# Gated linear attention with a top-1 expert layer on one core: the floor of a decay total moved into its scan, and two small VectorE operations moved to GpSimd

## The chip, the core and the metric

One core of one Trainium2 chip runs the whole program: attention, routing and the expert layer. The metric is device time in microseconds (us) of one launch. Engines are named as in the profile: PE is TensorE, PEld its weight loads, DVE VectorE, ACT ScalarE, POOL GpSimd, SP SyncE, from which most DMAs are issued.

## The reference

```
q, k, v, alpha: (4, 8, 768, 48) float32        # alpha between 0.8 and 1.0
for t in range(768):
    state = alpha[:, :, t, :, None] * state + k[t] (outer) v[t]     # 48 x 48 per head
    y[:, :, t] = q[t] @ state
x = y rearranged to (3072 tokens, 384)
logits = x @ w_gate (384 x 8) + modality_bias[modality_id]
e = argmax(logits);  gate = softmax(logits)[e]
out = gate * (relu(x @ w1[e]) @ w2[e])         # w1: 384 x 1024, w2: 1024 x 384, 8 experts
```

## The kernel before

**Attention in chunks.** The 3072 tokens are 24 chunks of 128: chunk `i` is batch `i // 6`, place `i % 6` in its sequence. A chunk holds all eight heads, laid out as four pairs of 48 rows padded to 64. Instead of stepping through time, the kernel takes within a chunk the running product of alpha and its reverse, scales k and q by them, and does the rest with matmuls. Between chunks of one batch a state `S` (four pairs of 48 x 48) is handed on.

**One loop, software pipelined.** Loop step `s` works on several chunks at once: `decay(s)`, `scale_k(s-1)`, `scale_q(s-1)`, `keys(s-2)`, `scores(s-2)`, `combine(s-3)`, `outputs(s-4)`, `rows(s-4)`. In the order of one step:

- `decay` (L236 on) runs on DVE. A scan backwards along time (L240) writes `G`: each element is x times the element before it in the scan, plus `DR`. `DR` is 0 except for a 1 at each of the five segment borders, where x is 0, so that the product starts again from 1. The first column of each of the four segments is the decay of the state over the whole chunk, the total. L244 writes these four totals, not below 1e-30, to `amin[:, i]`; L245 takes their reciprocal into `d`; L246 is the forward scan `Fw`, started from it.
- `scale_k` (L262) and `scale_q` (L268) multiply transposed k and q, read from PSUM, by `G` and `Fw` on DVE.
- `scores` (L277) multiplies them on PE, ACT copies the result to `scT` (L281), and POOL zeroes the future half in place with two affine selects (L282).
- `combine`: if the chunk isn't the first of its batch, L304 writes `U` (tiles `UB0` and `UB1` in turn), the state `S` times the totals in `G`. Then PE runs three runs of matmuls into one PSUM tile `y`: L324 (`U` by q), L330 (new k by v, for the state), L334 (scores by v). L338 then makes the next state on DVE, `S = U + ` the new part. L340 is the same for the first chunk of a batch.
- `outputs` (L347, ACT) copies `y` to `yt`; `rows` (L357 on PE, L361 and L362 on ACT) turns it and writes it to DRAM; `logits_turned` (L369) and `logits` (L378, L380) make the expert logits for two chunks at a time.

**Routing** for groups of finished chunks (`GROUPS`) runs between them on DVE with small matmuls (L433 to L477). Two experts are fixed early, after 16 and 18 chunks (`route_early`, L539 to L578): DVE writes the expert's number to `meta` (L545), SP reads it and issues the 3 MB of that expert's weights (`w1r`, `w2r`), and POOL gathers 256 token rows (`xg`, L679) and their gates (`gg`, L684) by indirect DMAs. The gates of the first 18 chunks go to DRAM as `gd` (L674) before they are gathered.

**Expert layer.** From about 170 us on, 12 slots of 256 tokens run: weights are split on ACT and DVE (L897, L899) into a high and a low part, and three matmuls take the place of one (L925 to L927, L948 to L950). POOL scatters the results.

**What sets the order.** A scheduler that works from a timeline of its own places the instructions of DVE and POOL from the dependencies; PE's matmuls in the later loop steps are pinned to the order in which they are written. Each engine then takes its list strictly from the front: an instruction that waits holds back all that stand behind it on that engine. POOL's list holds the affine selects and the indirect DMAs.

`out_of_range` (L698) reads all of `amin` after the last `decay`, and a fallback runs if a total is under 1e-17.

Of the kernel before, what the change touches and what calls it, by code (L numbers as in the profile page):

```python
# [14 lines left out]
ALU = mybir.AluOpType  # L15
# [7 lines left out]
B, H, S, D = 4, 8, 768, 48  # L23
NC = S // P
NP = H // 2
SEG = P + 1
# [22 lines left out]
AFLOOR = 1.0e-30  # L49
# [5 lines left out]
def attention_moe(ctx: ExitStack, tc: tile.TileContext, q, k, v, alpha, mid, wg, mb, w1, w2, out):  # L55
    nc = tc.nc
    vec, act, pool, pe, sp = nc.vector, nc.scalar, nc.gpsimd, nc.tensor, nc.sync
# [63 lines left out]
    def pin(ins):  # L121

        if mark.get("pin"):
            tc.keep_in_program_order(ins)
        return ins
# [24 lines left out]


    DR = ac.tile([P, NP * SEG + 1], F32, name="DR")
    vec.memset(DR, 0.0)
    vec.memset(DR[:, SEG :: SEG], 1.0)
    X, DF, UB = [], [], []
    for i in range(2):
# [12 lines left out]
    amin = ac.tile([P, NU, NP], F32, name="amin")  # L169
# [66 lines left out]
    def decay(i):  # L236
        x, d = X[i % 2], DF[i % 2]
        Fw = sb.tile([P, NP * SEG], F32, name="Fw", bufs=3)
        G = sb.tile([P, NP * SEG + 1], F32, name="G", bufs=4)
        vec.tensor_tensor_scan(  # L240
            G[:, 1:][:, ::-1], x[:, 1:][:, ::-1], DR[:, 1:][:, ::-1], 0.0, op0=ALU.mult, op1=ALU.add
        )
        ac1 = amin[:, i]
        vec.tensor_scalar(ac1, G[:, 1::SEG], AFLOOR, None, op0=ALU.max)  # L244
        vec.reciprocal(d[:, 0::SEG], ac1)  # L245
        vec.tensor_tensor_scan(Fw, x[:, :-1], d, 0.0, op0=ALU.mult, op1=ALU.add)  # L246
        st[i, "G"], st[i, "F"] = G, Fw

# [47 lines left out]
    def combine(i):  # L296
        c = i % NC
        qh, vt, sc = st[i, "q"], VT[i % NV], st[i, "s"]
        U = UB[i % 2]
        halves = [slice(64 * g, 64 * g + 64) for g in range(2)]  # L300
        if c > 0:
            S0 = st[i, "S"]
            A = st[i, "G"][:, 1::SEG].unsqueeze(2).broadcast_to([P, NP, D])
            vec.tensor_tensor(U[:, :, :D], S0, A, op=ALU.mult)  # L304

        yk = ps.tile([P, 2, 512], F32, name="y")

        def y(r, j):
            return yk[r, j % 2, P * (j // 2) : P * (j // 2 + 1)]

        kv = yk[:, 1, 2 * P : 2 * P + NP * D].rearrange("p (j d) -> p j d", j=NP)
        fresh = {(o, g) for o in range(2) for g in range(2)}

        def first(o, g):
            new = (o, g) in fresh
            fresh.discard((o, g))
            return new

        if c > 0:
            for a in range(2):  # L320
                for o in range(2):
                    for g in range(2):
                        x, j = g ^ o, 2 * a + o
                        pin(pe.matmul(y(halves[x], j), U[halves[g], j], qh[halves[g], j], start=first(o, x), stop=False))  # L324
        if c < NC - 1:
            kn = st[i, "n"]
            for h in range(H):
                j = h // 2
                r = halves[h % 2]
                pin(pe.matmul(kv[r, j], kn[:, j, r], vt[:, h, :D], start=first(1, h % 2), stop=False))  # L330
        for j in range(NP):
            for x, r in enumerate(halves):
                g = x ^ j % 2
                pin(pe.matmul(y(r, j), vt[:, 2 * j + g], sc[g][:, j], start=first(j % 2, x), stop=(j > 1)))  # L334
        if c < NC - 1:
            S1 = sb.tile([P, NP, D], F32, name="S")
            if c > 0:
                vec.tensor_tensor(S1, U[:, :, :D], kv, op=ALU.add)  # L338
            else:
                vec.tensor_copy(S1, kv)  # L340
            st[i + 1, "S"] = S1
        st[i, "yp"] = yk
# [454 lines left out]
    for s in range(NU + 3):  # L797
# [16 lines left out]
        if s < NU:  # L814
            decay(s)
# [25 lines left out]
        if 0 <= s - 3 < NU:  # L841
            combine(s - 3)
# [242 lines left out]
```

## Time and profile before

| what | us |
|---|---|
| median of 3 runs | 410.47 |
| lowest and highest | 408.89, 410.51 |
| the profiled execution | 408.91 |
| its span, first to last instruction | 407.1 |
| attention with most of the routing | 0 to about 170 |
| expert layer | about 170 to 400 |

The profiled execution is one run: its time is 1.81 us more than its span, which is what lies around the first and last instruction. Line numbers are those of the kernel before. A row of the timeline reads: start in us from the span's start, duration in us, engine, line, operation, output and inputs, shape, count, and in brackets how long the engine was idle before it and what released it. A row of the groups gives total busy us and mean ns of one, and after the second bar the idle time before. A row of the stages gives a stretch, its length, each engine's busy time and count, then the granted TensorE clock, the DMA share and GB/s.

### The profile page before, as it was taken

To read this page: it belongs to the slowest core of one execution; us is meant where nothing else is said; L and a number is where in the kernel's file an instruction comes from. 1 tells how busy PE (TensorE), PEld (TensorE's weight loads), DVE (VectorE), ACT (ScalarE), POOL (GpSimd) and SP (SyncE) were. 2 spreads that over 40 slices of the span, in tenths; PEclk is the share of its full clock that TensorE was granted. 3 is DMA by queue.
4 is the path that set the end of the run, shared out by engine and by line. 5 is a ranking of instruction groups with operands and counts; after the bars stand their busy time and mean duration, and the time that the engine had idled before them with its cause. 6 is when DMAs were issued, how large, how long until landed. Compare 5 with 4: busy or idle time off the path is not lost. (4 is left out here: it accounts for less than half of the span.)

```text
span 407.1 us, 9558 instructions
## 1 busy us (share of the span) xinstructions
PE 378.2 (93%) x3659; PEld 347.7 (85%) x3659; DVE 278.2 (68%) x550; ACT 224.3 (55%) x425; POOL 137.3 (34%) x175
## 2 busy tenths in 40 slices
PE   3898999999999888899997999999999999999992
PEld 3777787788778666778997999999999999999992
DVE  6787889878979965587689566665656666554230
ACT  3467677567566435344586657475654656545230
POOL 9321321321222233402657515244351634232010
PEclk9999999999999989999998999999999999999998
DMA  6999988579675096505999786566867657420010
GB/s 129 209 202 214 201 184 192 127 165 199 138 160 117 26 360 210 204 22 163 385 370 331 252 283 202 198 220 203 268 197 264 210 195 238 148 106 35 6 42 10
DMA packets 132655, 75.12 MB, mean 185 GB/s; under 512 B 103777, under 2 KB 120222, under 8 KB 132600
## 3 DMA queue, kind: packets, MB, share of 16 engines
q1 hardware_dynamic: 128504, 64.57, 56.6%
q0 software_dynamic: 4096, 9.85, 7.0%
q8 instruction: 31, 0.51, 0.5%
q14 instruction: 24, 0.20, 0.1%
HBM read 64.95 MB, written 9.65 MB: 183 GB/s over the span
## 5 line engine op out<-in xcount | busy, mean ns | idle before, releaser
L925 PE MATMUL tr<-xH,w1H 128*128 128x256 f32 x264 | 74.7, 286 | 1.3 <-DVE hL L932 1.3
L926 PE MATMUL tr<-xL,w1H 128*128 128x256 f32 x264 | 75.1, 285 | 0.0
L927 PE MATMUL tr<-xH,w1L 128*128 128x256 f32 x264 | 74.9, 285 | 0.0
L282 POOL TENSOR_SCALAR_AFFINE_SELECT scT<-scT 128x512 f32<-128x512 f32 x48 | 35.2, 754 | 107.1 <-ACT scT L281 107.1
L948 PE MATMUL sc<-w2H,hH 128*128 128x384 f32 x192 | 65.4, 342 | 1.0 <-ACT hH L929 1.0
L949 PE MATMUL sc<-w2L,hH 128*128 128x384 f32 x192 | 64.6, 337 | 0.0
L899 DVE TENSOR_TENSOR w2L<-w2r,w2H 128x768 fp32r<-128x768 f32 x52 | 49.1, 956 | 21.9 <-ACT w2H L897 21.0
L950 PE MATMUL sc<-w2H,hL 128*128 128x384 f32 x192 | 63.6, 340 | 0.0
L866 POOL DMA_INDIRECT out_dram<-os,odx x24 | 27.6, 1148 | 89.2 <-ACT os L953 34.9
L899 DVE TENSOR_TENSOR w1L<-w1r,w1H 128x768 fp32r<-128x768 f32 x44 | 41.7, 956 | 21.3 <-ACT w1H L897 20.6
L897 ACT CAST w1H<-w1r 128x768 fp32r<-128x768 f32 x44 | 36.0, 834 | 29.8 <-PE tr L926 23.0
L925 PEld LDWEIGHTS tr<-xH,w1H 128*128 128x128 f32 x264 | 50.9, 194 | 1.6 <-issue 1.6
L926 PEld LDWEIGHTS tr<-xL,w1H 128*128 128x128 f32 x264 | 51.2, 194 | 0.0
L927 PEld LDWEIGHTS tr<-xH,w1L 128*128 128x128 f32 x264 | 51.1, 194 | 0.0
L679 POOL DMA_INDIRECT xg<-xd,idx x26 | 32.0, 1230 | 42.5 <-PE y L887 36.5
L897 ACT CAST w2H<-w2r 128x768 fp32r<-128x768 f32 x52 | 42.2, 834 | 7.0 <-PE sc L950 6.8
L932 DVE SCALAR_TENSOR_TENSOR hL<-tr,hH 128x512 fp32r<-128x512 f32 x46 | 31.5, 686 | 10.5 <-ACT hH L929 7.2
L948 PEld LDWEIGHTS sc<-w2H,hH 128*128 128x128 f32 x192 | 36.1, 188 | 2.4 <-ACT hH L929 1.2
L929 ACT ACTIVATE hH<-tr 128x512 fp32r<-128x512 f32 x46 | 27.4, 595 | 16.2 <-PE tr L927 12.7
L684 POOL DMA_INDIRECT gg<-gd,idx x26 | 30.9, 1187 | 15.8 <-DMA gd<-gs 8.5
L949 PEld LDWEIGHTS sc<-w2L,hH 128*128 128x128 f32 x192 | 36.1, 188 | 0.0
L950 PEld LDWEIGHTS sc<-w2H,hL 128*128 128x128 f32 x192 | 36.0, 188 | 0.0
(218 smaller groups left out, 703.9 us busy)
## 6 DMA issues: line engine op xcount, KB each, us to landing
w1r<-in_moe_w_dram SPq DMA_DIRECT2D x26, 768.0 KB
w2r<-in_moe_w_dram SPq DMA_DIRECT2D x26, 768.0 KB
nat_a<-in_alpha_dram SPq DMA_DIRECT2D x24, 192.0 KB
nat_k<-in_k_dram SPq DMA_DIRECT2D x24, 192.0 KB
nat_q<-in_q_dram SPq DMA_DIRECT2D x24, 192.0 KB
vt<-in_v_dram SPq DMA_DIRECT2D x24, 192.0 KB
xd<-xs SPq DMA_DIRECT2D x24, 192.0 KB
xg<-xd,idx POOLq DMA_INDIRECT x26
```

What stands on the lines that cost most here:

```text
L282: pool.affine_select(s, s, [[0, NP], [1, P]], ALU.is_ge, 0.0, base=0, channel_multiplier=-1)
L679: pool.indirect_dma_start(xg[i % NX][:, u], None, xd[0:rows], ix, bounds_check=rows - 1, oob_is_err=False)
L684: pool.indirect_dma_start(gg[i % NX][:, u : u + 1], None, gd[0:rows], ix, bounds_check=rows - 1, oob_is_err=False)
L897: act.copy(hi, src)
L899: vec.tensor_tensor(lw, src, hi.bitcast(F32), op=ALU.subtract)
L925: pe.matmul(hp[:, z], wH[:, d, fs], xH[:, d], start=(d == 0), stop=False)
L926: pe.matmul(hp[:, z], wH[:, d, fs], xL[:, d], start=False, stop=False)
L927: pe.matmul(hp[:, z], wL[:, d, fs], xH[:, d], start=False, stop=(d == ND - 1))
L932: mark[f"h{j}L"] = vec.scalar_tensor_tensor(hL, hp, 0.0, hH.bitcast(F32), op0=ALU.max, op1=ALU.subtract)
L948: pe.matmul(op, hH[:, z, us], wH[:, z], start=(f == 0), stop=False)
L949: pe.matmul(op, hH[:, z, us], wL[:, z], start=False, stop=False)
L950: pe.matmul(op, hL[:, z, us], wH[:, z], start=False, stop=(f == NF - 1))
```

## The change

The background of `DR` becomes 1e-30 instead of 0 and the second operation of the first scan a maximum instead of an addition, so that `G` itself never falls below the floor. L244 goes: the reciprocal reads the four totals from `G`, and POOL copies them to `amin`. The product `U` in `combine` is made by POOL instead of DVE.

```diff
     DR = ac.tile([P, NP * SEG + 1], F32, name="DR")
-    vec.memset(DR, 0.0)
+    vec.memset(DR, AFLOOR)
     vec.memset(DR[:, SEG :: SEG], 1.0)
...
         vec.tensor_tensor_scan(
-            G[:, 1:][:, ::-1], x[:, 1:][:, ::-1], DR[:, 1:][:, ::-1], 0.0, op0=ALU.mult, op1=ALU.add
+            G[:, 1:][:, ::-1], x[:, 1:][:, ::-1], DR[:, 1:][:, ::-1], 0.0, op0=ALU.mult, op1=ALU.max
         )
-        ac1 = amin[:, i]
-        vec.tensor_scalar(ac1, G[:, 1::SEG], AFLOOR, None, op0=ALU.max)
-        vec.reciprocal(d[:, 0::SEG], ac1)
+        vec.reciprocal(d[:, 0::SEG], G[:, 1::SEG])
+        pool.tensor_copy(amin[:, i], G[:, 1::SEG])
         vec.tensor_tensor_scan(Fw, x[:, :-1], d, 0.0, op0=ALU.mult, op1=ALU.add)
...
             A = st[i, "G"][:, 1::SEG].unsqueeze(2).broadcast_to([P, NP, D])
-            vec.tensor_tensor(U[:, :, :D], S0, A, op=ALU.mult)
+            pool.tensor_tensor(U[:, :, :D], S0, A, op=ALU.mult)
```

The lists of PE, ACT and SP hold the same instructions in the same order as before. Lines behind the edit have one number less in the new kernel. The lists of DVE and POOL change; three places follow, with buffer numbers, by which a tile's rows can be told apart.

DVE in the middle of attention, before (`UB` is the state times the totals, `kh` and `qh` the scaled k and q):

```order
L338 TENSOR_TENSOR S_741<-UB1_160,y_716 128x192
L304 TENSOR_TENSOR UB0_154<-S_741,G_461 128x4x48
L262 TENSOR_TENSOR kh_754<-tr_755,G_657 128x512
L240 SCALAR_TENSOR_TENSOR G_769<-X1_156,DR_147 128x516
L268 TENSOR_TENSOR qh_761<-tr_762,Fw_656 128x512
L244 TENSOR_SCALAR amin_165<-G_769 128x4
L245 RECIPROCAL DF1_158<-amin_165 128x4
L246 SCALAR_TENSOR_TENSOR Fw_768<-X1_156,DF1_158 128x516
```

And DVE at the same place in the new kernel:

```order
L337 TENSOR_TENSOR S_741<-UB1_160,y_716 128x192
L261 TENSOR_TENSOR kh_754<-tr_755,G_657 128x512
L240 SCALAR_TENSOR_TENSOR G_769<-X1_156,DR_147 128x516
L267 TENSOR_TENSOR qh_761<-tr_762,Fw_656 128x512
L243 RECIPROCAL DF1_158<-G_769 128x4
L245 SCALAR_TENSOR_TENSOR Fw_768<-X1_156,DF1_158 128x516
```

Two of eight instructions have left DVE; the order of the other six is kept.

POOL at the end of attention, before (`scT_2384`, `scT_2387` belong to chunk 21, `scT_2516`, `scT_2519` to chunk 22, `scT_2625`, `scT_2628` to chunk 23; `xg` and `gg` are the gathers for the two early experts):

```order
L282 AFFINE_SELECT scT_2384<-scT_2384 128x512
L679 DMA xg0_116<-xd_60,idx_214 128x384 x2
L282 AFFINE_SELECT scT_2387<-scT_2387 128x512
L684 DMA gg0_119<-gd_61,idx_214 128x1 x2
L282 AFFINE_SELECT scT_2516<-scT_2516 128x512
L282 AFFINE_SELECT scT_2519<-scT_2519 128x512
L282 AFFINE_SELECT scT_2625<-scT_2625 128x512
L679 DMA xg1_117<-xd_60,idx_214 128x384 x2
L684 DMA gg1_120<-gd_61,idx_214 128x1 x2
L282 AFFINE_SELECT scT_2628<-scT_2628 128x512
```

And POOL at the same place in the new kernel, where the products with `G_2122`, `G_2223` and `G_2346` are those of chunks 21, 22 and 23:

```order
L678 DMA xg0_116<-xd_60,idx_214 128x384 x2
L281 AFFINE_SELECT scT_2387<-scT_2387 128x512
L683 DMA gg0_119<-gd_61,idx_214 128x1 x2
L303 TENSOR_TENSOR UB1_160<-S_2468,G_2122 128x4x48
L281 AFFINE_SELECT scT_2516<-scT_2516 128x512
L281 AFFINE_SELECT scT_2519<-scT_2519 128x512
L303 TENSOR_TENSOR UB0_154<-S_2586,G_2223 128x4x48
L281 AFFINE_SELECT scT_2625<-scT_2625 128x512
L678 DMA xg1_117<-xd_60,idx_214 128x384 x2
L683 DMA gg1_120<-gd_61,idx_214 128x1 x2
L281 AFFINE_SELECT scT_2628<-scT_2628 128x512
L303 TENSOR_TENSOR UB1_160<-S_2700,G_2346 128x4x48
```

The product of chunk 21 stands behind both gathers of gates `gg0`, that of chunk 22 behind the selects of its own scores, and that of chunk 23 behind four gathers and the last select.

## The prediction

> **What bounds the kernel now.** I read the stage table first, with stretches cut where PE begins a chunk's transposes, then the timeline of stretches where PE isn't full. Three chunks of attention and its end:
>
> ```profile
> 78.91:85.06 6.15, 5.86 (x90) 4.58 (x88) 4.62 (x8) 3.65 (x9) 1.62 (x3) 1.00 0.73 161
> 101.77:108.75 6.98, 6.60 (x102) 5.25 (x100) 6.70 (x18) 4.25 (x10) 2.18 (x4) 1.00 0.68 146
> 132.36:139.22 6.86, 6.15 (x89) 5.16 (x87) 6.79 (x20) 3.27 (x7) 2.17 (x4) 1.00 0.08 30
> 139.22:150.64 11.42, 8.72 (x115) 6.82 (x113) 8.49 (x40) 4.23 (x10) 4.24 (x5) 0.87 0.74 256
> 170.35:180.22 9.87, 9.87 (x64) 8.17 (x62) 6.19 (x15) 6.42 (x13) 0.00 (x0) 1.00 0.10 35
> ```
>
> The columns behind the length are PE, PEld, DVE, ACT, POOL. In a plain chunk (first row) PE is busy 5.86 of 6.15 us and DVE 4.62: DVE has 1.5 us to spare, and taking work from it buys nothing. In chunks with routing DVE is busy 6.70 of 6.98 and 6.79 of 6.86: there DVE sets the pace, and PE has holes. Behind attention PE is full again (last row), so a microsecond won or lost before 170 us reaches the end. So I followed the chunks with routing and the end of attention.
>
> **The price on DVE.** One chunk with routing:
>
> ```profile
> 103.11 0.34 DVE L338 TENSOR_TENSOR S<-UB,y 128x192 f32<-128x192 f32 x1
> 103.49 0.59 ACT L347 COPY yt<-y 128x512 f32<-128x512 f32 x1 [0.45 <-DVE S L338]
> 103.49 0.36 DVE L304 TENSOR_TENSOR UB<-S,G 128x192 f32<-128x192 f32 x1
> 103.77 0.68 DVE L262 TENSOR_TENSOR kh<-tr,G 128x512 f32<-128x512 f32 x1
> 104.13 0.64 PE L369 MATMUL rt<-yt,wgp 128*32 128x256 f32 x8 [0.38 <-ACT yt L347]
> 106.09 0.16 DVE L244 TENSOR_SCALAR amin<-G 128x4 f32<-128x4 f32 x1
> 106.28 0.18 DVE L245 RECIPROCAL DF<-amin 128x4 f32<-128x4 f32 x1
> 111.25 0.63 PE L357 MATMUL tr<-ident,yt 128*128 128x128 f32 x4 [0.29 <-DVE kh L262]
> ```
>
> Start to start, S to kh takes 0.66 us; with the product gone kh follows S by the 0.28 that it now follows the product, so **0.38 us** leave DVE. The maximum L244 costs 106.28 - 106.09 = **0.19 us**. Both fall on the path only where DVE has no idle time. Here S comes 0.2 earlier (one maximum stands between it and the last idle of DVE), yt and so PE's L369 by as much (its wait is 0.38); one chunk later kh comes 0.38 + 0.19 + 0.2 earlier, more than the 0.29 that PE's L357 waits for it. That is 0.2 + 0.3 = 0.5 us of PE per routing group, and the group at 66 us looks alike: **-1.0 us** for the two. In the other chunks kh waits for PE's transposes anyway: the product leaves and nothing moves.
>
> The scan keeps 1.23 us: it still has a multiplication and a dependent second operation, like L246. No row shows one with a maximum; the bounds are 0.68 (one pass over as much data, kh) and twice 1.23, and I take 1.23 since the two scans shown agree to 11 ns.
>
> ```profile
> L246 DVE TENSOR_TENSOR_SCAN Fw<-X,DF 128x516 f32<-128x516 f32 x24 | 29.8, 1242 | 0.7
> L240 DVE TENSOR_TENSOR_SCAN G<-X,DR 128x516 f32<-128x516 f32 x24 | 29.5, 1231 | 3.1 <-ACT X L232 3.0
> ```
>
> **The price on POOL.** 24 copies of four columns and 20 products go to an engine that sits idle 107.1 us ahead of the selects:
>
> ```profile
> L282 POOL TENSOR_SCALAR_AFFINE_SELECT scT<-scT x48: 632/638/1304, 16.1 to 167.8; 128x512 f32<-128x512 f32 x48
> masks.py:199 POOL TENSOR_SCALAR_AFFINE_SELECT ident<-ident 128x128 f32<-128x128 f32 x1 | 0.3, 284 | 0.0
> L187 POOL TENSOR_TENSOR tok<-tok,tge 128x24 f32<-128x24 f32 x1 | 0.2, 234 | 0.1
> ```
>
> A copy of four columns costs no more than L187's 0.23 us; its readers come a whole loop later, so it is free. A product on 128x192 has two inputs. From 284 ns at 128 columns and 638 at 512 one input costs 0.92 ns a column; two inputs, twice that: 234 + 168 x 1.84 = 543 ns, say **0.6 us** with its start. Bounds: 0.23 (L187) and 1.30 (the slowest select). In a plain chunk that is hidden: S is ready at 79.37, PE reads U at 82.97 (rows below), 3.6 us later.
>
> ```profile
> 79.02 0.35 DVE L338 TENSOR_TENSOR S<-UB,y 128x192 f32<-128x192 f32 x1 [0.59 <-PE y L334]
> 82.97 0.67 PE L324 MATMUL y<-qh,UB 64*64 64x128 f32 x16
> 22.39 1.50 DVE L246 TENSOR_TENSOR_SCAN Fw<-X,DF 128x516 f32<-128x516 f32 x1
> 6.41 1.04 POOL L505 CAST zc<-zi 128x1 f32<-128x1 int32 x1
> ```
>
> The last two rows show that DVE's scans and POOL's work hold each other up: a scan beside a select took 1.50 instead of 1.23, a cast of one column beside a scan 1.04. The Trainium skill says so too ("SBUF — State Buffer", "Who interferes with whom": a DVE instruction with two SBUF inputs and a GpSimd one that reads SBUF exclude each other, and whichever starts first keeps the port). By that rule it speaks against this change: in dense chunks the new product would still run when the next G scan is due, and the sum would be worse by some 0.2 us a dense chunk. From the rows alone: S to G is 0.88 us without the product, the product ends 0.35 + 0.1 + 0.6 = 1.05 behind S's start, a delay of 0.17 to a scan whose result PE wants a step later. I put it at 0 and keep 0.2 x 4 = 0.8 for the range.
>
> **The end of attention, where the product is queued.** POOL's list puts the product of chunk 21 behind the two gathers of gates, and that of chunk 23 behind four gathers and a select:
>
> ```profile
> 139.97 0.14 DVE L545 TENSOR_SCALAR meta<-base 1x1 int32<-1x1 f32 x1
> 146.50 0.17 PE L453 MATMUL rt<-oh,tri 128*128 128x16 bf16 x1 [1.44 <-DVE vals L529]
> 148.77 1.94 PE L334 MATMUL y<-scT,vt 128*64 128x128 f32 x16
> 153.84 1.01 POOL L684 DMA_INDIRECT gg<-gd,idx  x1 [3.95 <-DMA gd<-gs]
> 155.16 1.00 POOL L684 DMA_INDIRECT gg<-gd,idx  x1 [0.30 <-issue]
> 154.85 0.67 PE L324 MATMUL y<-qh,UB 64*64 64x128 f32 x16
> 157.21 0.88 PE L118 MATMUL sc<-ident,xg 128*128 128x128 f32 x6
> 157.90 0.35 DVE L338 TENSOR_TENSOR S<-UB,y 128x192 f32<-128x192 f32 x1
> 167.75 0.64 POOL L282 TENSOR_SCALAR_AFFINE_SELECT scT<-scT 128x512 f32<-128x512 f32 x1
> 168.72 0.67 PE L324 MATMUL y<-qh,UB 64*64 64x128 f32 x16
> ```
>
> POOL waits for `gd` to land until 153.84, and its gathers end at 156.16. The product then takes 0.05 + 0.6, and 0.1 until PE sees it: L324 of chunk 21 can't start before 156.92 unless `gd` lands earlier; now it starts at 154.85. `gd` lands when the weights queued ahead of it are through (the DMA share, rows below, is about 1 to 152.8 and 0 from 153.6), and these follow `meta` at 139.97. DVE ahead of `meta` has no idle time from 128 us on: it loses two maxima and one product, 0.19 + 0.38 + 0.19, with rounding 0.85, so `gd` moves by -1.0 - 0.85 and L324 to 156.92 - 1.85 = **155.07, +0.2**. PE itself would be there far sooner: L453 needn't wait its 1.44, since the scan ahead of L529 ends some 1.7 us earlier. So PE stands still for about 3 to 4.6 us, and what DVE won there is lost.
>
> That standstill has a price of its own. Behind the holes at 141 and 145 us the granted clock fell:
>
> ```profile
> 145.60:146.40 0.80, 0.00 (x0) 1.00 1.05 410
> 147.20:148.00 0.80, 0.80 (x19) 0.78 1.06 399
> 148.00:148.80 0.80, 0.80 (x18) 0.50 1.08 394
> 150.40:151.20 0.80, 0.80 (x7) 0.59 1.08 378
> 152.00:152.80 0.80, 0.80 (x10) 1.00 0.88 342
> 153.60:154.40 0.80, 0.64 (x12) 1.00 0.00 0
> 147.19 0.76 PE L324 MATMUL y<-qh,UB 64*64 64x128 f32 x16
> 147.58 0.71 SPq L674 DMA_DIRECT2D gd<-gs  x2
> ```
>
> (In the stage rows PE alone, then clock, DMA share, GB/s.) L324 to the end of L334 took 150.71 - 147.19 = 3.52 us at 0.50 instead of 157.28 - 154.85 = 2.43 at 1.00 (L334 ends 0.07 behind L118's start): 1.1 us. The longer hole at 152 should bring it again, perhaps not over the whole piece: **+0.8**. The Trainium skill ("TensorE: Matmul & The Clock Gate", "What's actually happening") has the clock halved after an idle window of about 3.4 us, with windows that run freely: by that rule a hole of 4.6 us always counts and one of 3 only by chance, so the sum is +0.9 or +0.1 below. The trace agrees in the length of the drop, 3.4 us.
>
> S of chunk 21 then starts at 155.07 + 2.43 + 0.1 + 0.8 = 158.4, now 157.90 (DVE's routing made it late): **+0.5**, which contains the terms so far. PE, ACT and POOL behind it move with it. Last, the product of chunk 23 comes behind the select that ends at 168.39: 0.05 + 0.6 + 0.1 give 169.14 for L324 instead of 168.72, **+0.4**. From there PE is full.
>
> **The sum.** +0.5 + 0.4 = **+0.9 us** against the profiled execution's 408.91, whose span of 407.1 has 1.81 around it that doesn't change. That execution is at the low end of the runs, 1.56 below their median; the three lie at 408.89, 410.47 and 410.51, a gap of the size of one clock drop. I add the 0.9 to their mean, 409.96: **410.8 us**. What a measurement can tell from no change is about 0.5%, 2.05 us, so this is no change.
>
> **The rivals.**
>
> *The hold on POOL is cheap (faster).* If `gd` lands a fixed 6.3 us after its issue at 147.58 and not behind the weights, it moves with PE, by 1.0 + 1.7, and PE hardly stands still; the clock drop at 147 goes as well. For it: the hole ahead of L453. Against: the DMA share falls to 0 just when gg starts. L324 of chunk 21 then starts about 0.7 earlier, S 1.2, the drop gives back up to 1.1 more, chunk 23 costs 0.4: -0.8 to -1.9; with all other dense chunks shorter by their full 0.57 rather than by PE's waits (four of them, about 1.2 more) -3: 407 to 409, middle 408.0. Chance 0.20.
>
> *POOL's queue costs all of it (slower).* If the gains ahead of `meta` don't reach PE, eaten by scans that POOL holds up, `gd` stays at 153.84: L324 at 156.92 is +2.07, at half clock 1.1 more, so S at 156.92 + 2.43 + 1.1 + 0.1 = 160.55, +2.65, then +0.4: +3.05, **413.0**. It decides as soon as less than about 0.9 of the 1.85 arrives. For it: 22.39 and 6.41 above; against: PE's waits on S and kh are there to be cut. Chance 0.18.
>
> *The scan with a maximum is slower*, up to 1.23 us each: hidden in plain chunks (4.62 + 1.23 - 0.57 of 6.15), but in eight dense ones on the path: up to +9.8, 420. No row speaks for it. Chance 0.03. That the change doesn't do what it says can be left out: the lists show both operations moved.
>
> **The numbers.** Forecast 0.59, from -1.5 to +2.0 about its own mean, 408.5 to 412.0; the rivals 0.20, 0.18, 0.03. Faster by over 0.5% (below 408.4): most of the first rival, 0.16, and 0.04 of the forecast's edge, 0.20. Slower (above 412.5): most of the second, 0.14, the third 0.03, an edge of 0.04: 0.21. Within: 0.59. The range takes in the product at its bounds (-0.4 and +0.7, twice), the scans and the clock drop, and reaches into both rivals: 407.9 to 413.2.
>
> **What would show it.** Right: L304's successor at about 0.6 us on POOL; DVE busy falls by about 11 us (20 x 0.37 + 24 x 0.16); S at the dense chunks 0.2 to 0.7 earlier; L324 of chunk 21 released by POOL after a hole of 3 us or more, and a granted clock of 0.5 behind it. Wrong: no wait of L324 on POOL; a product of over 1.3 us; a scan G other than 1.23; or a time that moves in the expert layer, where no instruction has changed.

## The result: 0.6% slower

The new kernel took 413.01 us, the median of 20 runs (408.27 to 416.20), the kernel before on the same chip 410.49 (406.66 to 413.88). The ratio is **1.0061, 95% interval 1.0035 to 1.0087**: about 2.5 us longer. Times in us are medians of all runs, while ratios and intervals leave out slow runs, those more than 1.5% above the fastest of their own kernel, so a ratio isn't the quotient of two medians. The profiled execution took 409.6 us with a span of 407.5, that is 3.4 below the median of its own kernel, against 408.91 and 407.1 for before. Whoever compares the two spans sees +0.4 and misses the change; it has to be read stretch by stretch.

From the page of the new kernel (its line numbers are one less than before behind the edit), the span, the engines and four groups:

```profile
span 407.5 us, 9586 instructions
PE 377.4 (93%) x3659; PEld 346.9 (85%) x3659; DVE 264.4 (65%) x506; ACT 224.0 (55%) x425; POOL 149.7 (37%) x219
L240 DVE TENSOR_TENSOR_SCAN G<-X,DR 128x516 f32<-128x516 f32 x24 | 29.5, 1230 | 5.5 <-ACT X L232 5.4
L245 DVE TENSOR_TENSOR_SCAN Fw<-X,DF 128x516 f32<-128x516 f32 x24 | 29.5, 1230 | 0.5
L303 POOL TENSOR_TENSOR UB<-S,G 128x192 f32<-128x192 f32 x20 | 10.3, 513 | 12.7 <-DVE S L337 11.3 <-DVE S L339 1.2
L244 POOL COPY amin<-G 128x4 f32<-128x4 f32 x24 | 5.5, 228 | 36.8 <-DVE G L240 36.7
```

The edit did what it says, at the prices expected: the scan with a maximum takes 1230 ns (1231 before), the product 513 ns on POOL, a copy 228 ns in the mean, and DVE has 264.4 us of work instead of 278.2.

Where the time went is seen with three markers that both kernels share: the G scan of chunk 9, that of chunk 22, and the first matmul behind the 1.00 us wait for `hH` in the expert layer. From the timelines, before first, then the new kernel:

```profile
56.06 1.22 DVE L240 TENSOR_TENSOR_SCAN G<-X,DR 128x516 f32<-128x516 f32 x1
135.05 1.22 DVE L240 TENSOR_TENSOR_SCAN G<-X,DR 128x516 f32<-128x516 f32 x1
217.36 0.44 PE L948 MATMUL sc<-w2H,hH 128*128 128x384 f32 x1 [1.00 <-ACT hH L929]
```

```profile
56.80 1.22 DVE L240 TENSOR_TENSOR_SCAN G<-X,DR 128x516 f32<-128x516 f32 x1
133.67 1.24 DVE L240 TENSOR_TENSOR_SCAN G<-X,DR 128x516 f32<-128x516 f32 x1
219.18 0.44 PE L947 MATMUL sc<-w2H,hH 128*128 128x384 f32 x1 [1.00 <-ACT hH L928]
```

Up to the first marker the new kernel loses 0.74 us; between the scans it **wins 2.12** (78.99 to 76.87); from the scan of chunk 22 to the expert layer it **loses 3.20** (82.31 to 85.51); behind that it wins 1.42 (189.74 to 188.32). The sum is +0.40, the difference of the spans. The first and the last of these four turn out to be chance (below, the table of all kernels); the two in the middle are the change. In these two executions the middle ones sum to +1.08 us, and the medians differ by 2.5, so 1.4 us of the loss isn't in this pair of profiles. A likely place is the clock: the mean granted clock was 0.986 in the profiled execution and 0.980 in the median of the 20 runs. A drop to half for 3.4 us takes 0.0042 off that mean, so a typical run had one or two drops more; where they lie isn't recorded.

The loss has its place. The timeline of the new kernel at the end of attention, the rows that answer to those of the prediction (what follows in brackets is idle time and what ended it):

```profile
138.39 0.14 DVE L544 TENSOR_SCALAR meta<-base 1x1 int32<-1x1 f32 x1
152.12 1.01 POOL L683 DMA_INDIRECT gg<-gd,idx  x1 [3.97 <-DMA gd<-gs]
153.43 1.00 POOL L683 DMA_INDIRECT gg<-gd,idx  x1 [0.30 <-DVE OHE L559]
154.45 0.52 POOL L303 TENSOR_TENSOR UB<-S,G 128x192 f32<-128x192 f32 x1
155.03 1.13 PE L323 MATMUL y<-qh,UB 64*64 64x128 f32 x16 [3.45 <-POOL UB L303]
156.98 1.94 PE L333 MATMUL y<-scT,vt 128*64 128x128 f32 x16
159.03 0.35 DVE L337 TENSOR_TENSOR S<-UB,y 128x192 f32<-128x192 f32 x1 [5.85 <-PE y L333]
170.03 0.51 POOL L303 TENSOR_TENSOR UB<-S,G 128x192 f32<-128x192 f32 x1
170.60 0.67 PE L323 MATMUL y<-qh,UB 64*64 64x128 f32 x16 [0.82 <-POOL UB L303]
```

`meta` came 1.58 us earlier than before, and the first gather that waits for `gd` 1.72 us. But POOL still sat 3.97 us for `gd`, and the product of chunk 21 stood behind both gathers: PE stood still for 3.45 us. What the holes then did, in the stage table (PE busy and its instructions, granted clock, DMA share, GB/s):

```profile
150.00:152.00 2.00, 1.06 (x17) 1.00 0.85 315
152.00:154.00 2.00, 0.00 (x0) 1.00 0.04 10
154.00:156.00 2.00, 0.97 (x16) 0.52 0.80 212
156.00:158.00 2.00, 2.00 (x30) 0.50 0.95 346
158.00:160.00 2.00, 2.00 (x16) 0.50 1.05 394
160.00:162.00 2.00, 2.00 (x18) 0.78 1.06 374
162.00:164.00 2.00, 2.00 (x52) 1.00 0.94 333
```

The clock lay at 0.50 from about 154.1 to 160.9 us, worked out from the partial rows: 6.8 us, twice the 3.4 of the drop before. S of chunk 21 came at 159.03 instead of 157.90, L323 of chunk 23 at 170.60 instead of 168.72, +1.88, and that is carried into the expert layer unchanged (+1.82 at the third marker). In each of these differences 0.74 us is the later arrival at chunk 9.

### The profile page after: what moved, and what is told of

Read it like the earlier page. It is cut to its first block, busy times and chain, and to the rows that moved or that the text cites. A ratio compares the mean times of both kernels' runs of the same rounds, so it can differ in the third digit from the quotient of the medians.

```text
span 407.5 us, 9586 instructions
## 1 busy us (share of the span) xinstructions
PE 377.4 (93%) x3659; PEld 346.9 (85%) x3659; DVE 264.4 (65%) x506; ACT 224.0 (55%) x425; POOL 149.7 (37%) x219
## 5 line engine op out<-in xcount | busy, mean ns | idle before, releaser
L281 POOL TENSOR_SCALAR_AFFINE_SELECT scT<-scT 128x512 f32<-128x512 f32 x48 | 32.6, 700 | 45.9 <-ACT scT L280 45.8
L683 POOL DMA_INDIRECT gg<-gd,idx x26 | 30.0, 1152 | 15.7 <-DMA gd<-gs 8.4
```

Of the source, the lines that this page charges most:

```text
L281: pool.affine_select(s, s, [[0, NP], [1, P]], ALU.is_ge, 0.0, base=0, channel_multiplier=-1)
L683: pool.indirect_dma_start(gg[i % NX][:, u : u + 1], None, gd[0:rows], ix, bounds_check=rows - 1, oob_is_err=False)
```

## The experiments

The theories: **A**, the loss is the place of the late products in POOL's list, behind gathers that wait for `gd`; **B**, products on POOL and scans on DVE hold each other up all along; **C**, the floor and the copies cost. Each kernel was timed in 12 runs against 35 or 36 of the kernel before on its chip; the medians of those were 408.08 us for the first four kernels below, 407.61 for the next four and 408.38 for the last four.

### One part of the change alone, or undone

The new kernel with all products back on VectorE:

```diff
-            pool.tensor_tensor(U[:, :, :D], S0, A, op=ALU.mult)
+            vec.tensor_tensor(U[:, :, :D], S0, A, op=ALU.mult)
```

> The new kernel with the product U back on VectorE; the floor in the scan and the copies of the totals on GpSimd are kept. Theory A (the loss comes from where the product stands in GpSimd's queue at the end of attention): that loss is gone and 24 maxima of 0.19 us have left VectorE, so 0 to 1.5 us faster than before, about 409.5. Theory B (GpSimd's product holds up the scans in the chunks with routing): the same here, since the product is gone; a copy of four columns is too short to matter. Theory C (the loss comes from the floor in the scan or from the copies): as slow as the new kernel, about 412.5.

Measured: 407.86 us, ratio **0.9952 [0.991, 0.9994]**. The floor and the copies cost nothing, so C falls. That they win is less sure: the two medians, 407.86 and 408.08, lie almost level.

The kernel before with only the product moved to GpSimd (the same line, the other way):

> The kernel before with only the product U moved to GpSimd. Theory A: the queue at the end of attention is as in the new kernel, so 412 to 414; the product of chunk 21 is released by GpSimd and TensorE stands still before it for 2.5 to 3.5 us. Theory B: 412 to 414 as well. Theory C: no slower than before, 409.5 to 410.5.

Measured: 412.26 us, **1.0100 [1.0057, 1.0142]**. The product carries the loss.

The new kernel with the last three of the twenty products back on VectorE:

```diff
-            pool.tensor_tensor(U[:, :, :D], S0, A, op=ALU.mult)
+            (vec if i > 20 else pool).tensor_tensor(U[:, :, :D], S0, A, op=ALU.mult)
```

> The new kernel with only the products of chunks 21, 22 and 23 back on VectorE; the other 17 stay on GpSimd. Theory A: no hold is left, and what VectorE won in the chunks with routing arrives: 1 to 3.5 us faster than before, 407 to 409.5, and the wait of 3.45 us ahead of chunk 21's first matmuls is gone. Theory B: 17 of 20 products still hold up scans: 411.5 to 412.5. Theory C: 411.5 to 412.5.

Measured: 406.58 us, **0.9925 [0.9881, 0.997]**, faster than both kernels. Seventeen products on POOL cost nothing, so B falls.

The kernel before with one product of twenty, that of chunk 21, on GpSimd:

```diff
-            vec.tensor_tensor(U[:, :, :D], S0, A, op=ALU.mult)
+            (pool if i == 21 else vec).tensor_tensor(U[:, :, :D], S0, A, op=ALU.mult)
```

> The kernel before with one product of twenty, that of chunk 21, on GpSimd, behind the two gathers of gates. Theory A: TensorE's matmuls of chunk 21 start at about 156.9 instead of 154.85 and run partly at half clock: 2 to 3 us slower than before, 412.5 to 413.5. Theory B and C: as before, 410 to 411, since one product and no floor is moved.

Measured: 410.59 us, **1.0063 [1.0026, 1.01]**: this single product costs as much as the whole change. Its timeline shows the same queue:

```profile
153.57 1.01 POOL L684 DMA_INDIRECT gg<-gd,idx  x1 [3.73 <-DMA gd<-gs]
154.89 1.00 POOL L684 DMA_INDIRECT gg<-gd,idx  x1 [0.30 <-issue]
155.91 0.52 POOL L304 TENSOR_TENSOR UB<-S,G 128x192 f32<-128x192 f32 x1
156.49 0.67 PE L324 MATMUL y<-qh,UB 64*64 64x128 f32 x16 [1.56 <-POOL UB L304]
```

A is what the four times say. In this kernel's profiled execution (408.7 us, again below its median) the clock didn't drop behind the hole, and the marker of the expert layer lies at 217.33, no later than before. The hold is in that profile all the same. Counted from the G scan of chunk 22, PE's first matmul of chunk 21 comes 1.69 us later than before (21.49 against 19.80) and that of chunk 22 0.92 later (27.57 against 26.65). It is made up at chunk 23, where the profile before is late by itself. S of chunk 22 waits there until 1.84 us behind the end of L334, and here 0.05 us (before first):

```profile
162.80 1.06 PE L334 MATMUL y<-scT,vt 128*64 128x128 f32 x16
165.70 0.35 DVE L338 TENSOR_TENSOR S<-UB,y 128x192 f32<-128x192 f32 x1 [2.61 <-PE rt L378]
```

```profile
163.67 1.06 PE L334 MATMUL y<-scT,vt 128*64 128x128 f32 x16
164.78 0.35 DVE L338 TENSOR_TENSOR S<-UB,y 128x192 f32<-128x192 f32 x1 [0.82 <-PE y L334]
```

The profile of the new kernel has that late S too (167.38, 1.86 us behind L333), and no other profile has it. The instructions around it stand in the same order; what held S isn't shown. So the whole stretch up to the expert layer is no clean measure against the kernel before.

### The hold, the clock, the order of the queue

Is the loss the waiting or the clock behind it? The new kernel with 24 transposes put on PE into the hold, whose results nobody reads:

```diff
+        if i == 21:
+            busy = ps.tile([P, NP, P], F32, name="rt")
+            for n in range(24):
+                pin(pe.transpose(busy[:, n % NP], ident, ident))
```

> The new kernel with 24 transposes of the identity into a spare PSUM tile ahead of chunk 21's first matmuls, so that TensorE works through most of the 3.45 us for which it waited; no result uses them. Theory A with a clock term (the hold costs TensorE its clock as well: 0.50 from 154 to 160.8 us): the matmuls behind the hold run at full clock, L323 to L333 takes about 2.4 us instead of 3.9, and the kernel is 1.5 to 2.5 us faster than the new kernel though it does more: about 0 to +0.3% against before. Theory A without it: as the new kernel, +0.6%. If the 24 transposes last longer than the hold, up to 0.5 us is lost again.

Measured: 407.80 us, **1.0001 [0.9967, 1.0036]**. Its timeline and stage table:

```profile
158.59 0.53 POOL L303 TENSOR_TENSOR UB<-S,G 128x192 f32<-128x192 f32 x1
158.66 2.84 PE L321 MATMUL rt<-ident 128*128 128x128 f32 x24 [0.24 <-DVE meta L548]
161.42 0.67 PE L327 MATMUL y<-qh,UB 64*64 64x128 f32 x16
```

```profile
156.00:158.00 2.00, 1.74 (x23) 1.00 0.04 8
158.00:160.00 2.00, 1.51 (x13) 1.00 0.29 99
160.00:162.00 2.00, 2.00 (x30) 1.00 0.59 114
```

Here the product ended at 159.12, and the useful matmul came 2.3 us later still, held by the filler. The profile is of this kernel's slowest run (412.28), with a drop from about 149 to 155 ahead of the rows. In it chunk 22's first matmul starts 29.69 us behind the G scan of chunk 22, as late as in the new kernel, so this profile shows no gain. Yet over its runs the kernel isn't slower than before. With the clock at 1.00, L327 took 0.67 us and not 1.13. Work that computes nothing won back the 0.6%, which points to the clock behind the wait rather than the wait itself, but doesn't show it. The intervals of this kernel and of the new one meet at 1.0035, and they come from two chips. Nor do the granted clocks of the runs settle it: their median is 0.980 in the new kernel, 0.984 here and 0.988 before on this chip, but 0.980 also in the two kernels with product 21 back and the gates moved, when timed again below, and these are level with the kernel before.

The kernel before with the product of chunk 23 alone on GpSimd (`i == 23` in the line above):

> The kernel before with one product of twenty, that of chunk 23, on GpSimd, behind four gathers and the last select. By the prediction's term +0.4 us (+0.1%); by the wait of 0.82 us which the new kernel shows there, +0.8 us (+0.2%). If this place is what costs most, +0.5% or more.

Measured: 408.47 us, **1.0017 [0.9979, 1.0055]**. PE waits 1.5 us for it, and no loss can be told from the kernel before. That doesn't make this wait free: the profile before is late at chunk 23 without it. PE's first matmul of chunk 23 comes 7.02 us behind that of chunk 22 before, 7.21 here, and 5.60 with product 21 alone on GpSimd.

The new kernel with product 21 alone on VectorE (`vec if i == 21 else pool`):

> The new kernel with only the product of chunk 21 back on VectorE; those of 22 and 23 stay on GpSimd. Against the kernel with all three back (-0.75%) it should lose what chunk 23 costs, 0.4 to 1 us: -0.5%. If the wait behind the gates is the whole loss, -0.75% as well; if chunk 23 is the larger part, 0 or slower.

Measured: 406.26 us, **0.9981 [0.994, 1.0021]**. The loss is gone although nineteen products stay on POOL and L323 of chunk 23 waits 1.6 us for the last. The gain is smaller than expected: it lies between the 0.5% of that forecast and the 0 named for the case that chunk 23 is the larger part.

The other way to take the hold away is to leave all twenty on POOL and move the gathers of gates behind product 21:

```diff
+            mark["U", i] = pool.tensor_tensor(U[:, :, :D], S0, A, op=ALU.mult)
...
+        with tc.issue_after(mark["U", 21].ins):
             for e in range(NA):
                 gather_gates(e, row(EARLY[e]))
```

> The new kernel with all twenty products on GpSimd, and only the two gathers of gates moved behind the product of chunk 21 in GpSimd's list. Theory A (what the product waits for is the gathers ahead of it, not GpSimd's speed): no wait ahead of chunk 21's matmuls, the clock stays, and the time is that of the kernel with only chunk 21 back: -0.4 to -0.75%. If the product were too slow on GpSimd or hurt the scans beside it: no better than the new kernel, +0.6%.

Measured: 409.69 us, **1.0034 [1.0001, 1.0067]**: slower than expected, a miss. The hold was gone (product 21 at 152.78, directly behind its state), but the profiled execution had another drop, ahead of it, also of 6.8 us:

```profile
146.00:148.00 2.00, 0.66 (x19) 0.85 0.99 358
148.00:150.00 2.00, 1.98 (x29) 0.50 1.05 399
150.00:152.00 2.00, 2.00 (x26) 0.50 1.06 373
152.00:154.00 2.00, 2.00 (x13) 0.50 1.06 395
```

### All late gathers behind the products, and three kernels again on one chip

To part the queue from a cost of later gathers, a kernel in which, beyond that, the four gathers of the second early expert stand behind product 23:

```diff
+    with tc.issue_after(mark["U", 23].ins):
+        gather(1, row(EARLY[1]))
+        gather_gates(1, row(EARLY[1]))
     outputs(NU - 1)
```

> All twenty products stay on GpSimd; in its list the gate gathers of the first early expert stand behind product 21, and all four gathers of the second early expert behind mask and product of chunk 23. Theory A (only the place in the list costs): both products start as soon as the state is there, L323 of chunk 21 and of chunk 23 wait under 0.8 us for UB, and the ratio to the kernel before is 0.988 to 0.998, as for the version with the last three products on VectorE. Theory D (a product on GpSimd at the end of the attention costs in itself, or a later gather does): 1.000 to 1.007, with the loss behind 160 us.

Measured: 406.06 us, **0.9941 [0.9898, 0.9984]**. All twenty products are on POOL, and none is waited for at the end of attention. Its timeline at chunk 21 and chunk 23:

```profile
150.18 0.52 POOL L303 TENSOR_TENSOR UB<-S,G 128x192 f32<-128x192 f32 x1 [1.21 <-DVE S L337]
152.95 1.03 POOL L683 DMA_INDIRECT gg<-gd,idx  x1 [2.26 <-DMA gd<-gs]
153.57 0.67 PE L323 MATMUL y<-qh,UB 64*64 64x128 f32 x16
163.26 0.52 POOL L303 TENSOR_TENSOR UB<-S,G 128x192 f32<-128x192 f32 x1 [1.21 <-DVE S L337]
164.06 1.03 POOL L678 DMA_INDIRECT xg<-xd,idx  x1 [0.28 <-issue]
166.15 0.67 PE L323 MATMUL y<-qh,UB 64*64 64x128 f32 x16
```

POOL waits for `gd` as before (2.26 us), but with the product ahead of the wait. This is the cleanest test of A: no instruction is taken back from POOL, only the order is another, and with it the start of the gathers. It takes away the wait at chunk 23 as well as that at chunk 21.

Beside it, the kernel with the gates moved, once more:

> The version with only the gate gathers moved behind product 21, once more, on the same chip as the other three. If its 1.0034 came from where the clock drops happened to fall, the ratio is now 0.992 to 0.999 and the interval of the stretch from the first meta to the second-layer row at about 217 us is at most 77.5 us in the profile. If the moved gathers themselves cost, 1.001 to 1.007 again.

Measured: 408.50 us, 1.0007 [0.9966, 1.0048], 76.45 us from `meta` (142.10) to the marker (218.55): the profile as expected of chance, the time between the two expectations. Whether moving only these gathers costs some 0.2% stays open.

> Product 21 alone on VectorE, beside the three others on one chip. Theory A: 0.994 to 1.001, and 0.5 to 1.5 us under the version with the gate gathers moved if those cost, level with it (0.3%) if not. If chunk 23's wait of 1.6 us counts, 0.2 to 0.5% over the version with the last three products on VectorE.

Measured: 407.97 us, 1.0013 [0.9971, 1.0056], just above what A expected, and level with the kernel before. It is also level with the gates moved, which speaks against a price of later gates, and 0.25% above the next kernel, within the 0.2 to 0.5% named for the case that the wait at chunk 23 counts.

> The last three products on VectorE, beside the three others on one chip. Theory A: 0.988 to 0.997, the lowest of the four or level with the version that moves all late gathers behind the products. If its 0.9925 was a matter of one chip, 0.998 to 1.002.

Measured: 408.34 us, 0.9988 [0.994, 1.0035]: above what A expected, within what was named for a matter of one chip. So its 0.9925 was partly luck; the mean of its two ratios is 0.9957.

### What the profiles of all kernels say together

For each profiled execution: start to the G scan of chunk 9, from there to that of chunk 22, from there to the marker in the expert layer, and the rest of the span (us), with the measured ratio. The kernel with the filler isn't listed, its marker can't be told apart.

| kernel | to chunk 9 | chunk 9 to 22 | to expert layer | rest | ratio |
|---|---|---|---|---|---|
| before | 56.06 | 78.99 | 82.31 | 189.74 | 1 |
| new | 56.80 | 76.87 | **85.51** | 188.32 | 1.0061 |
| product alone | 59.16 | 77.35 | **84.68** | 189.81 | 1.0100 |
| product 21 alone | 56.47 | 78.53 | 82.33 | 189.67 | 1.0063 |
| product 23 alone | 60.30 | 78.91 | 82.45 | 188.24 | 1.0017 |
| floor and copies alone | 59.29 | 77.99 | 81.10 | 189.82 | 0.9952 |
| last three back | 57.31, 58.08 | 76.83, 76.82 | 80.89, 80.95 | 188.17, 189.75 | 0.9925, 0.9988 |
| product 21 back | 56.34, 58.98 | 76.78, 76.94 | 81.92, 79.73 | 188.26, 189.85 | 0.9981, 1.0013 |
| gates moved | 59.73, 60.56 | 76.97, 76.82 | 82.79, 81.17 | 189.81, 189.75 | 1.0034, 1.0007 |
| all gathers moved | 57.42 | 77.07 | 80.26 | 189.75 | 0.9941 |

Read by columns. The second is the same within 0.3 us in all eight profiles that have every edit up to there (76.78 to 77.07), and 78.53 to 78.99 in the three that have none: **the gain of about 1.9 us is real**, some 0.8 of it from floor and copies. The third is above 84 in the two kernels with all products on POOL in the plain order, and 79.7 to 82.8 in all others. The first and the last scatter between executions of one kernel (56.34 and 58.98; 188.17 and 189.75), so neither the +0.74 nor the -1.42 of the result is the change.

Split at PE's first matmuls of chunk 22 and chunk 23, the third column shows both holds. Up to chunk 22 it takes 27.57 to 29.69 us in the three kernels whose product 21 stands behind the gathers, and 23.92 to 26.99 in the other ten profiles. From there to chunk 23 it takes 7.21 to 7.24 us where product 23 stands behind the gathers, 7.02 in the kernel before, whose late S was shown above, and 5.60 or 5.61 in the rest. Of these 1.6 us the kernels with product 23 on VectorE lose about 0.55 again behind it, and the one with all gathers moved loses nothing.

The ratios agree in kind. The kernels with every edit, no hold at chunk 21 and the one at chunk 23 kept (product 21 back, gates moved) have a mean ratio of 1.0009 over four measurements, where the new kernel has 1.0061: the hold at chunk 21 costs some 0.5%, 2.1 us. The kernels with neither hold (last three back, all gathers moved) have 0.9951 over three, another 0.6%, of which the profiles show 1.1 to 1.6 us. These differences are hardly larger than one interval and come from several chips, so their sizes are rough.

## Why the prediction was nearly right

The forecast was +0.9 us, "no change", 410.8; measured were +2.5 us and 413.0. That lies at the upper end of the stated range of 407.9 to 413.2, and not within the 0.5% that had the chance of 0.59, but in the part above 412.5 that had 0.21. Half a us of the miss is the base, 410.49 where 409.96 stood. Point by point:

- **The price on DVE, -1.85 us at `meta`: right in kind, too small by half a us.** `meta` came 1.58 earlier, but 2.32 earlier counted from chunk 9 (138.39 - 56.80 against 139.97 - 56.06). Up to the G scan of chunk 21 it was 1.56 (71.04 against 72.60) where -1.0 stood, and from there to `meta` 0.76 (10.55 against 11.31) where -0.85 stood. DVE lost 13.8 us of work, where 11 had been worked out.
- **The scan at 1.23, the copy free, the product at 0.6: right.** 1230, 228 and 513 ns.
- **Scans and products hold each other up, put at 0: right.** The G scan's mean is 1230 against 1231 ns, the Fw scan's 1230 against 1242. The rule of the Trainium skill that was weighed there ("SBUF — State Buffer", "Who interferes with whom") shows on the other side: one of the 24 copies of four columns, beside a G scan, took 1163 ns where the typical one takes 187. The copies are off the path.
- **The hold at chunk 21, L323 at 155.07 behind a hole of 3 to 4.6 us: right in its mechanism, with luck in the time.** 155.03, 3.45 us, released by the product. Counted from chunk 9, though, L323 came 0.56 earlier than before (98.23 against 98.79) and not 0.2 later: the larger gain on DVE and the start that was 0.74 late by chance cancel.
- **The clock drop, +0.8: the step that failed, by its size.** L323 to the end of L333 took 158.92 - 155.03 = 3.89 us, 1.46 over the 2.43 at full clock, and the drop went on to 160.9. I had taken one drop of 3.4 us, the length seen before, "perhaps not over the whole piece"; it lasted 6.8. S came 1.13 late and not 0.5. And that a hole of 4.6 us always counts doesn't follow from the rule that was given: it contains a whole window of 3.4 us only if the two line up, and a hole of 3 us never does. In the profiles the clock fell without a whole idle window: PE was busy for 1.71 of the 3.41 us ahead of the drop before, and for 0.40 in the new kernel.
- **Chunk 23, +0.4: its mechanism right, its size not to be told from this pair.** L323 was released by the product, 0.57 us behind its start at 170.03. But the whole was +1.88 where +0.9 stood: 0.63 from S, the other 0.35 I put down to the half clock that lasted into chunk 22. Counted from chunk 9 the whole is +1.14 (113.80 against 112.66), close to the +0.9, because the larger gain and the larger drop nearly cancel; that is luck. And the time before to which this term was added, 168.72, contains the late S of chunk 22: against the kernels without this hold it costs 1.1 to 1.6 us.
- **The rest of the span unchanged: right for the change**, though the two profiles differ there by 1.42 us. I had named time that moves in the expert layer as proof against me; the repeated kernels show that it moves there with nothing changed.
- **The rivals.** "The hold on POOL is cheap" fell with the 3.45 us wait. "POOL's queue costs all of it", 413.0, has the time that was measured but not the reason: it needs gains that don't arrive at `gd`, and L324 at 156.92; they arrived. The scan with a maximum cost nothing.

What the working lacked was the pair of drops: the drop at 147 us, one window, that before has, is gone in the new profile (L333 of chunk 20 takes 1.06 us instead of 1.94), and that wins nothing, because PE then waits for POOL anyhow; the new one, behind the hold, falls on work that is on the path.

## What to carry to other kernels

An operation that is moved to an idle engine takes a place in that engine's list, and the engine's share of busy time says nothing about that place: read what stands ahead of it, above all transfers that wait for a landing, and move either the few operations that are late there or the gathers behind them (here 0.9941 with the order alone, where the plain move gave 1.0061 on another chip). Price a new standstill of TensorE at its wait plus the half clock behind it, and count that as up to two of the drops already in the trace: behind the product of chunk 21, waits of 1.56, 2.10 and 3.45 us brought no drop, one of 3.4 us and one of 6.8. Where executions of one kernel scatter by more than the change, compare profiles between markers that both share, put against them the same kernel profiled twice, and see whether the kernel that you compare with is late there by itself.

## What the runs showed of the hardware that was not expected

- A hole of 3.45 us brought 6.8 us at half clock, where a shorter one had brought 3.4. A likely reason, argued and not shown: the clock fell at 154.1, while PE still stood still until 155.03, so the stretch of 3.4 us that began there was not a busy one either. The Trainium skill ("TensorE: Matmul & The Clock Gate", "What's actually happening") has the clock come back after at least one busy window of about 3.4 us, and windows that run freely; the trace agrees if it is the next whole window that counts. That isn't all of it: of the five drops of two windows in the profiles, the one at 33.9 to 40.7 us in the repeat of the gates moved had PE busy throughout both.
- Twenty-four transposes that nobody uses, 2.84 us of PE, put into a wait cost nothing in the time (1.0001 against 1.0061 without them, on another chip).
- In the expert layer, where no kernel differs, the rest of the span has two values, 188.2 to 188.3 and 189.7 to 189.9, in executions of the same kernel. In all thirteen profiles of the table it goes with one drop: the nine with 189.7 to 189.9 have 3.4 us at half clock between 217 and 228 us, the other four have none, so one drop costs 1.5 us there. The granted clock behind the waits at the marker tells them apart in the two executions of the kernel with the last three products back, over 217 to 227 us (first the one at 188.17, then that at 189.75):

```profile
217.00:227.00 10.00, 9.70 (x62) 1.00 0.87 310
```

```profile
217.00:227.00 10.00, 8.88 (x49) 0.83 0.93 342
```

- A profile can hide a loss that it contains: product 21 alone measured 1.0063 and looks like the kernel before in all four stretches, though its chunk 21 starts 1.69 us late, because the profile before is late at chunk 23.
